# Attention with a Schraudolph-style exponent on VectorE: one of its four shifted lines made by DMA transfers inside SBUF

## The chip, the cores and the metric

The kernel runs on one core of a Trainium2 chip. The metric is the time of one execution on the device, in microseconds (us). Three executions of the kernel before took 676.72, 677.89 and 678.13 us, so the median is 677.89 us. A further execution was profiled: it took 677.84 us, and its span, from the first to the last instruction of the program, is 675.9 us.

Engine names are those of the profile: PE is TensorE (matrix multiply), ACT is ScalarE, DVE is VectorE, POOL is GpSimd and SP is SyncE, which here only issues DMA transfers. PEld is the weight load of PE.

## The reference

Attention without a mask over 32 heads, 2048 queries and keys, and 20 numbers per head. Queries and keys are normalised, a temperature per head scales the logits, and all is bf16:

```python
qn = q / (jnp.sqrt((q * q).sum(axis=-1, keepdims=True)) + eps)
kn = k / (jnp.sqrt((k * k).sum(axis=-1, keepdims=True)) + eps)
logits = jnp.einsum('bhqd,bhkd->bhqk', qn, kn) * t[None, :, None, None]
attn = _softmax(logits, axis=-1)
return jnp.einsum('bhqk,bhkd->bhqd', attn, v)
```

q, k and v are (1, 32, 2048, 20), t is (32). Since the logits are bounded by t, no maximum is subtracted: the kernel computes exp(logit) for each pair, multiplies it with v, and divides by the sum, which comes from a column of ones beside v.

## The kernel before, in words

**Tiles.** The work is cut into units: one head, 128 keys (on the partitions) and 512 queries (on the free axis). There are 32 heads x 16 key blocks x 4 query blocks = 2048 units. Four heads make a group (8 groups), a group and a query block make a superblock (32 superblocks of 64 units). PE makes the logits of a unit in a PSUM bank of 128 x 512, an engine takes the exponent and writes it to SBUF in 16 bits, and PE multiplies that tile with v into the accumulator `psO`.

**Two ways to an exponent.** A unit goes one of two ways.

- An *A unit* goes to ACT. PE puts two or three units ("a wave") into `psA`, and one ACTIVATE (line 867) writes exp of all of them into `pA`. A unit costs PE one multiplication with v.
- A *D unit* goes to DVE (and POOL). Line 313 (`P1`) multiplies and adds a constant and writes int16 to `dI`, so that the bits read as float16 are roughly an exponential. Three more lines of the same unit, `dS1`, `dS2` and `dS3`, are `dI` plus an integer constant each (`SHIFTS`; the constant of `dS3` is 565 - 123 = 442). The four readings, with `dI` counted once whole and once half through `vhalf`, are summed by PE in `psO`, and their errors cancel. A D unit costs PE five multiplications with v.

In the kernel before 1448 units are A units and 600 are D units. D units do not start before 12% of the work is issued (`D_FROM`).

**The shifts.** `shift_op` (line 318) makes a shifted line on DVE (line 328, up to four tiles of 512 in one instruction, `RUN_MAX`) or on POOL (line 326, 512 int16 as 256 int32, or two tiles at once). POOL is given only `dS1` (`POOL_S` = 1); DVE makes all of `dS2` and `dS3` and what POOL does not reach of `dS1`. `dI` and `dS1` to `dS3` are rings of 20 tiles (`RING`).

**The order of work.** A planner in the kernel (`make_plan`, line 423) plays the execution before it is built: it has a cost for each instruction, lets each engine take the ready piece of work of the best priority, and writes down the order of every engine. That order is fixed in the program; the engines meet only through semaphores. What is an A unit and what a D unit comes out of this play: `step_qkd` (line 916) starts a D unit when a bank of `psD` is free and no more than 24 shifts are waiting (`D_WAIT`). Two neighbouring `P1` are joined into one instruction if 12 or more shifts are waiting (`JOINB`, line 1035). If PE is used little, it gets filler multiplications (line 542) that add zeros.

The planner keeps POOL and DVE apart. Every DVE operation is marked `port` unless it is one of `P1`, `cp`, `drain`, `red`, `inv`, `rec` (line 207); `step_pool` (line 1052) starts a POOL instruction only while a DVE instruction without that mark runs, and only if it fits into it; a POOL instruction sets `lock`, until which DVE takes no marked one. An operation with `alone` set (line 1056) is exempt: it starts on POOL as soon as it is ready, and sets no lock.

SP issues its transfers in its order too: loads of q, k, v (80 KB to 320 KB), transposes of the padded q and k inside SBUF (`tr_op`, line 394: 128 rows of 4 KB, so 512 KB), and stores of the output.

Of the kernel before, what the change touches and what calls it, by code (L numbers as in the profile page):

```python
# [10 lines left out]
I16 = mybir.dt.int16  # L11
# [5 lines left out]
SHIFTS = (123, 382, 860, 565)  # L17
# [9 lines left out]
WAVES = (3, 2)  # L27
NPA = 14
RING = 20
RUN_MAX = 4  # L30
RUN_MIN = 4
D_FROM = .12
D_END = 14
D_LAST = 14
# [98 lines left out]
def bass_standalone__qk_norm__prompt_kernel(  # L133
# [12 lines left out]
    NSB = HG * QG  # L146
    QW = 512

    with ExitStack() as es:
        sbuf = lambda name, shape, dt: es.enter_context(nc.sbuf_tensor(name, shape, dt))  # L150
        sem = lambda name: es.enter_context(nc.semaphore(name))
# [10 lines left out]
        qpad = [sbuf(f"qpad{i}", [128, R, NH, 32], BF16) for i in range(2)]  # L162
# [6 lines left out]
        dI = sbuf("dI", [128, RING * QW], I16)  # L169
        dS = [dI] + [sbuf(f"dS{i}", [128, RING * QW], I16) for i in range(1, len(SHIFTS))]  # L170
        zt = sbuf("zt", [128, QW], BF16)
        shc = sbuf("shc", [128, len(SHIFTS)], I32)
        nrc = sbuf("nrc", [128, 4], F32)
        iot = sbuf("iot", [128, 128], F32)
        idn = sbuf("idn", [128, 128], BF16)
        nr0 = sbuf("nr0", [128, 2, NH, 4], F32)
# [17 lines left out]
            return dma_sems[nsem[0] - 1]  # L194

        n_sq = [0]

        def ap(tile, base, *dims):
            return bass.AP(tile, base.offset, [base.ap[0]] + [list(d) for d in dims])
# [118 lines left out]
        def shift_op(eng, i, j, n):  # L318
# [3 lines left out]
            if eng == "POOL":  # L322
# [4 lines left out]
            return dve(f"S{i}", n * QW, R4,  # L327
                       lambda e: e.tensor_single_scalar(o, x, float(SHIFTS[i] - SHIFTS[0]), ALU.add), rd, wr)  # L328

        def half_op(hg):  # L330
            b = hg % 2
            f = lambda tl: tl[b][:, :, :, :].rearrange("p h r d -> p (h r d)")
            return dve("vh", NH * R * 32, R4, lambda e: e.tensor_single_scalar(f(vhalf), f(vaug), 0.5, ALU.mult),  # L333
                       [("v", b, hh) for hh in range(NH)] + [("vz", b)], [("vh", b)])
# [88 lines left out]
        def make_plan(share):  # L423

            P = Plan()
            nsem[0] = n_sq[0] = 0
            SWITCH, PEL, SEML = 0.11, 0.18, 0.06
            units_of = lambda sb: {hh: [(sb, hh, r) for r in range(R)] for hh in range(NH)}
            pool = {sb: units_of(sb) for sb in range(NSB)}
            left = lambda sb: sum(len(x) for x in pool[sb].values())  # L430
# [18 lines left out]
            seq = [0]  # L449
            lock = [0.0]  # L450
            sp_todo = []
            pool_todo = []
            pending_pv = []
            shifts = []
            pe_mode, grp, pe_t = None, [0.0] * 4, 0.0

            def ready_at(op):
# [59 lines left out]
            o = P.link(load_qk(0, 0, 0)[0])  # L517
# [19 lines left out]
                    want_dve(o, 1.5)  # L537
            for o in zeros(1, [("qpad", 0, 0)]):
                want_dve(o, 5)

            def heat_mm(bank, n):
                return lambda e: e.matmul(bank, zt[:, 0:128], zt[:, 0:n], start=False, stop=False, skip_group_check=True)  # L542
# [38 lines left out]
            for r0, r1, a0, a1 in ((4, 16, 1, 2), (4, 16, 0, 1)):  # L581
# [28 lines left out]
            def progress():  # L610
                return (issued_a + issued_d) / float(R * NH * QG)
# [16 lines left out]
            def feed_prep():  # L628
                while next_prep:
                    pr, o = next_prep[0]  # L630
                    if pr is None:
                        for w_ in ("k", "q"):
                            x = tr_op(o, w_, 0, R)
                            x.reads.append((w_ + "z", o % 2))
                            want_sp(x)
                        next_prep.pop(0)
                        continue
                    if progress() < pr:
                        break
                    want_dve(o, PRIO)  # L640
                    next_prep.pop(0)
# [274 lines left out]
            def step_qkd(used, with_a):  # L916
                nonlocal a_sb, d_sb, issued_d, d_over
                if d_over or progress() < D_FROM:
                    return False
                d_sb = a_sb  # L920
                if a_sb == NSB or a_sb == NSB - 1 and left(a_sb) < D_END:
                    d_over = True
                    return False
                while d_sb < NSB - 1 and left(d_sb) < D_LAST:
                    d_sb += 1
                if d_sb == NSB - 1 and left(d_sb) < D_END or left(d_sb) < D_LAST:
                    return False
                if pe_mid:
                    return False
                def empty(i):  # L930
                    rds = P.readers.get(("psD", i), [])
                    return all(r.done is not None and r.done + SEML <= now for r in rds) and (rds or P.last_w.get(("psD", i)) is None)
                pb = issued_d % 2
                if not empty(pb):
                    return False
                n = 2 if not pb and left(d_sb) > 1 and empty(1) else 1
                if len(shifts) > D_WAIT:
                    return False
                j = issued_d % RING
                old = [(nm, j + t_) for t_ in range(n) for nm in ["dI"] + [f"dS{i}" for i in range(1, len(SHIFTS))]]  # L940
                if any(x[3] in old for x in pending_pv):
# [12 lines left out]
                pe_group("QKD", [qk_mm(u, psD[:, (pb + i) * QW:(pb + i + 1) * QW]) for i, u in enumerate(us)], "qk",  # L954
                         [kk for u in us for kk in qk_keys(u)], [("psD", pb + i) for i in range(n)], [u[1] for u in us])
                p1s = [p1_op(pb + t_, j + t_, 1) for t_ in range(n)]
                for t_, p1 in enumerate(p1s):
                    want_dve(p1, PRIO1)
                    for i in range(1, len(SHIFTS)):

                        shifts.append((issued_d - n + t_, i, j + t_, 1, p1))
                for t_, u in enumerate(us):
                    for i, cs in enumerate(COEF):
                        nm = f"dS{i}" if i else "dI"
                        x = dS[i][:, (j + t_) * QW:(j + t_ + 1) * QW].bitcast(F16)
                        for c in cs:
                            pending_pv.append((p1s[t_] if i == 0 else Later(nm, j + t_, issued_d), u, x, (nm, j + t_), c != 1))
                return True

            def step_act():  # L970
                nonlocal n_act
# [141 lines left out]
            while True:  # L1113
                moved = True
                while moved:
                    moved = False
                    feed_prep()
                    if loaded < HG and progress() > loaded - 1 + (0.02 if loaded > 1 else 0.2) and cur >= (loaded - 1) * QG:
# [172 lines left out]
```

## Time and profile before

| what | value |
|---|---|
| median of three executions | 677.89 us |
| profiled execution | 677.84 us |
| span of the profiled execution | 675.9 us |
| granted TensorE clock | 0.996 |
| ACT busy | 662.3 us (98%) |
| DVE busy | 657.4 us (97%) |
| PE busy | 653.6 us (97%) |
| POOL busy | 345.6 us (51%) |
| mean busy share of the DMA engines, queue q1 | 18.6% |

The busy time of an engine is the union of its instructions; a matmul's end is modelled, so PE's share is not a measure of its peak. A row of the groups gives the line of the code, the engine, the operation, what it writes and reads, shapes, the count, then the busy time in us and the mean duration in ns (durations of neighbours overlap a little, so busy divided by count is what one more costs), then the idle time in front of the group and what ended it. The page also follows the chain of work that ended last back from the end, and gives its shares by engine and line.

### The profile page before, as it was taken

To read this page: it belongs to the slowest core of one execution; us is meant where nothing else is said; L and a number is where in the kernel's file an instruction comes from. 1 tells how busy PE (TensorE), PEld (TensorE's weight loads), DVE (VectorE), ACT (ScalarE), POOL (GpSimd) and SP (SyncE) were. 2 spreads that over 40 slices of the span, in tenths; PEclk is the share of its full clock that TensorE was granted. 3 is DMA by queue.
4 is the path that set the end of the run, shared out by engine and by line. 5 is a ranking of instruction groups with operands and counts; after the bars stand their busy time and mean duration, and the time that the engine had idled before them with its cause. 6 is when DMAs were issued, how large, how long until landed. Compare 5 with 4: busy or idle time off the path is not lost.

```text
span 675.9 us, 17317 instructions
## 1 busy us (share of the span) xinstructions
PE 653.6 (97%) x7454; PEld 214.0 (32%) x7454; DVE 657.4 (97%) x1049; ACT 662.3 (98%) x587; POOL 345.6 (51%) x533
## 2 busy tenths in 40 slices
PE   8999999999999999999999999999999999999996
PEld 4433323323333222232323232323232323232232
DVE  7999999999999999999999999999999999999994
ACT  6999999999999999999999999999999999999996
POOL 3364455454654545545355545655456554546652
PEclk8999999999999999999999999999999999999999
DMA  6500133005130043000530014300133001100000
GB/s 68 86 7 1 33 73 39 1 2 102 9 33 1 13 92 20 21 2 10 94 21 21 1 33 72 21 21 2 32 57 35 22 1 36 30 7 16 2 11 15
DMA packets 113778, 19.66 MB, mean 29 GB/s; under 512 B 102944, under 2 KB 113696, under 8 KB 113696
## 3 DMA queue, kind: packets, MB, share of 16 engines
q1 hardware_dynamic: 112896, 18.37, 18.6%
q8 instruction: 60, 0.98, 0.6%
q10 hardware_dynamic: 800, 0.12, 0.1%
q14 instruction: 22, 0.18, 0.1%
HBM read 7.87 MB, written 2.62 MB: 16 GB/s over the span
## 4 chain that ended last, share of the span: by engine, by line
ACT 68%; PE 25%; DVE 6%; DMA 0%; issue 0%; POOL 0%; DVEq 0%
ACT pA L867 68%; PE psO L696 11%; PE psA L674 8%; PE psO L542 3%; PE psD L674 3%; DVE dI L313 3%; DVE dS L328 1%; DMA qk<-in_q_dram 0%; DVE ssum L247 0%; DVE accT L348 0%; DVE vhalf L333 0%; DVE sqs L244 0%; DVE qpad L292 0%; DVE rn L279 0%; POOL kpad L292 0%
## 5 line engine op out<-in xcount | busy, mean ns | idle before, releaser
L867 ACT ACTIVATE pA<-psA 128x1536 bf16<-128x1536 f32 x579 | 658.1, 1323 | 3.7 <-PE psA L674 3.1
L326 POOL TENSOR_TENSOR dS<-dI,shc 128x256 int32<-128x256 int32 (+1 forms) x369 | 265.5, 723 | 223.4 <-DVE dS L328 170.6
L313 DVE TENSOR_SCALAR dI<-psD 128x512 int16<-128x512 f32 (+1 forms) x414 | 370.8, 916 | 3.7 <-PE psD L674 1.3
L674 PE MATMUL psA<-qT,kT 32*128 32x512 bf16 x1724 | 250.1, 383 | 12.4 <-ACT pA L867 9.4
L696 PE MATMUL psO<-dS,vaug 128*32 128x512 f16 x1800 | 248.5, 383 | 0.0
L696 PE MATMUL psO<-pA,vaug 128*32 128x512 bf16 x1448 | 242.9, 384 | 0.0
L328 DVE TENSOR_SCALAR dS<-dI 128x2048 int16<-128x2048 int16 (+3 forms) x366 | 227.3, 644 | 0.0
L674 PE MATMUL psD<-qT,kT 32*128 32x512 bf16 x600 | 167.9, 381 | 2.0 <-DVE dI L313 1.1
L696 PE MATMUL psO<-dI,vaug 128*32 128x512 f16 x600 | 136.6, 385 | 0.5 <-DVE accT L348 0.5
L696 PE MATMUL psO<-dI,vhalf 128*32 128x512 f16 x600 | 134.9, 382 | 0.0
L674 PEld LDWEIGHTS psA<-qT,kT 32*128 32x128 bf16 x1724 | 62.0, 91 | 207.7 <-ACT pA L867 187.2
L696 PEld LDWEIGHTS psO<-dS,vaug 128*32 128x32 bf16 x1800 | 65.1, 95 | 91.6 <-issue 65.0
L696 PEld LDWEIGHTS psO<-pA,vaug 128*32 128x32 bf16 x1448 | 62.0, 94 | 44.4 <-issue 27.7
L542 PE MATMUL psO<-zt 128*128 128x128 bf16 x659 | 64.1, 225 | 0.0
L542 PEld LDWEIGHTS psO<-zt 128*128 128x128 bf16 x659 | 40.3, 99 | 40.4 <-issue 40.0
L674 PEld LDWEIGHTS psD<-qT,kT 32*128 32x128 bf16 x600 | 37.2, 91 | 28.6 <-DVE dI L313 18.5
L292 POOL TENSOR_TENSOR qpad<-qk,rn 128x160 bf16<-128x160 bf16 x56 | 24.8, 459 | 35.6 <-DVE dS L328 27.6
L292 POOL TENSOR_TENSOR kpad<-qk,rn 128x160 bf16<-128x160 bf16 (+1 forms) x57 | 25.6, 463 | 32.2 <-DVE dS L328 28.6
L696 PEld LDWEIGHTS psO<-dI,vaug 128*32 128x32 bf16 x600 | 34.2, 94 | 23.2 <-issue 11.6
L696 PEld LDWEIGHTS psO<-dI,vhalf 128*32 128x32 bf16 x600 | 34.8, 95 | 14.9 <-issue 10.8
L354 POOL TENSOR_TENSOR ost<-accT,rec 128x320 bf16<-128x320 f32 x31 | 23.7, 766 | 25.8 <-DVE dS L328 22.6
L348 DVE STREAM_TRANSPOSE accT<-psO 128x512 f32<-128x512 f32 x32 | 22.5, 702 | 5.4 <-PE psO L696 5.4
(54 smaller groups left out, 114.6 us busy)
## 6 DMA issues: line engine op xcount, KB each, us to landing
vaug<-in_v_dram SPq DMA_DIRECT2D x32, 80.0 KB, 4.1
qk<-in_k_dram SPq DMA_DIRECT2D x7, 320.0 KB, 4.4
out_dram<-ost SPq DMA_DIRECT2D x28, 80.0 KB, 1.9
qk<-in_q_dram SPq DMA_DIRECT2D x6, 320.0 KB, 4.3
qk<-in_q_dram SPq DMA_DIRECT2D x4, 80.0 KB, 3.2
out_dram<-ost SPq DMA_DIRECT2D x7, 40.0 KB, 2.0
qk<-in_k_dram SPq DMA_DIRECT2D x1, 240.0 KB, 3.7
qk<-in_q_dram SPq DMA_DIRECT2D x1, 240.0 KB, 4.3
```

What stands on the lines that cost most here:

```text
L292: emit = lambda e, o=dst, x=src, s=sc: e.tensor_tensor(o, x, s, ALU.mult)
L313: lambda e: e.tensor_scalar(dst, psD[:, pb * QW:(pb + n) * QW], 1024.0 * LOG2E, 15360.0 - 1024.0 * LOG2K + SHIFTS[0], ALU.mult, ALU.add),
L326: lambda e: e.tensor_tensor(o.bitcast(I32), x.bitcast(I32), c, ALU.add), rd + ["shc"], wr)
L328: lambda e: e.tensor_single_scalar(o, x, float(SHIFTS[i] - SHIFTS[0]), ALU.add), rd, wr)
L348: dve("drain", QW, R1, lambda e: e.transpose(aT[:, :, :].rearrange("p b d -> p (b d)"), psO[:, :]), ["psO"], [("accT", b)]),
L354: pool_op("omul", 320, True, lambda e: e.tensor_tensor(dst, num, rcb, ALU.mult), [("accT", b), ("rec", b)], [("ost", ob, qg)]) if pool else
L542: return lambda e: e.matmul(bank, zt[:, 0:128], zt[:, 0:n], start=False, stop=False, skip_group_check=True)
L674: return lambda e: e.matmul(dst, lhsT, rhs, tile_position=(32 * hh, 0))
L696: return lambda e: e.matmul(dst, lhsT, rhs, start=first, stop=last, skip_group_check=True, tile_position=(0, 32 * hh))
L867: a = Op("ACT", "exp", lambda e, s=src, d=dst: e.activation(d, s, ACT.Exp), [("psA", slot)], [("pA", pslot, i) for i in range(WAVES[slot]) ...
```

## The change

The line `dS3` of most D units is no longer made by DVE. For each batch of four neighbouring tiles of the ring (`DB` = 4):

1. `set`: SP issues a transfer SBUF to SBUF that copies `cadd`, a tile of 128 x 2048 int16 filled once with the constant 442, over the four tiles of `dS3`. It can run as soon as the old contents of the tiles have been read.
2. `far`: once the four tiles of `dI` are written and `set` has landed, POOL issues a transfer SBUF to SBUF that adds `dI` onto those four tiles (`accum_op=ALU.add`).

A batch is made so if at least 24 units are left in the superblock (`DMA_LEFT`) and it is not the last one; otherwise DVE makes `dS3` as before. `far` is `alone`: the planner lets POOL issue it whenever it is ready. The planner counts `DMA_POOL` for the issue and `DMA_LAT` until it lands, and 4.0 for `set` (figures written in the code, see the diff, not measurements). PE's multiplications with `dS3` of these tiles wait for the semaphore of `far`.

Since the planner plays the work with the new costs, the whole order comes out anew. By the instructions of the two programs (the branch that runs):

| instructions | before | after |
|---|---|---|
| A units / D units | 1448 / 600 | 1424 / 624 |
| ACTIVATE of 3 / 2 / 1 units | 290 / 289 / 0 | 285 / 284 / 1 |
| `P1` of one tile / of two | 228 / 186 | 510 / 57 |
| DVE shifts of 4 / 3 / 2 / 1 tiles | 291 / 31 / 33 / 11 | 169 / 46 / 72 / 51 |
| POOL shifts of one tile / of two | 272 / 97 | 307 / 26 |
| `set` on SP, `far` on POOL | 0 | 126 each, all of four tiles |
| PE multiplications with `dI`, `dS` and `pA` | 4448 | 4544 |
| PE filler multiplications (line 542 before) | 659 | 315 |

So 504 of the 624 tiles of `dS3` come from transfers.

```diff
+DB = 4
+DMA_POOL = 1.05
+DMA_LAT = 4.0
+DMA_LEFT = 24
+DMA_EVERY = 1
+DMA_ALONE = True
...
+        cadd = sbuf("cadd", [128, DB * QW], I16)
...
+        def shared(o, name, j):
+
+            k = (name, j // DB)
+            if k not in ring_sems:
+                ring_sems[k] = sem(f"s_{name}{j // DB}")
+            ring_val[k] = ring_val.get(k, 0) + 16
+            o.sem, o.val = ring_sems[k], ring_val[k]
+            return o
+
+        def far_op(j, n):
+            i = len(SHIFTS) - 1
+            sl = slice(j * QW, (j + n) * QW)
+            o = Op("POOL", "far", lambda e: e.dma_start(dS[i][:, sl], dI[:, sl], accum_op=ALU.add), [("dI", j + t_) for t_ in range(n)] + [("set", j)],
+                   [(f"dS{i}", j + t_) for t_ in range(n)], DMA_POOL, DMA_POOL + DMA_LAT)
+            o.alone = DMA_ALONE
+            return shared(o, "far", j)
+
+        def set_op(j, n):
+            i = len(SHIFTS) - 1
+            sl = slice(j * QW, (j + n) * QW)
+            return shared(Op("SP", "set", lambda e: e.dma_start(dS[i][:, sl], cadd[:, 0:n * QW]), ["cadd"],
+                             [("set", j)] + [(f"dS{i}", j + t_) for t_ in range(n)], 0.1, 4.0), "set", j)
...
+            if share:
+                want_dve(Op("POOL", "z", lambda e: e.memset(cadd[:, :], SHIFTS[-1] - SHIFTS[0]), [("qpad", 0, 0)], ["cadd"], 1.8, 1.9), 5)
...
                 for t_, p1 in enumerate(p1s):
                     want_dve(p1, PRIO1)
-                    for i in range(1, len(SHIFTS)):
+                    batch = (issued_d - n + t_) // DB
+                    if (j + t_) % DB == 0:
+                        far[0] = left(d_sb) >= DMA_LEFT and d_sb < NSB - 1 and batch % DMA_EVERY == 0 and RING % DB == 0
+                        if far[0]:
+                            want_sp(set_op(j + t_, DB))
+                    elif far[0] and lates and lates[0][1] != d_sb or d_sb == NSB - 1:
+                        far[0] = False
+                    if far[0]:
+                        lates.append((j + t_, d_sb))
+                    for i in range(1, len(SHIFTS) - far[0]):
...
+            def feed_far():
+                while lates and (len(lates) >= DB or not far[0] or left(lates[0][1]) < D_LAST):
...
+                    o = P.link(far_op(j, k))
...
+                    pool_todo.append([0, seq[0], o])
+                    del lates[:k]
```

More of the change, by code (lines that the diff above doesn't have):

```diff
@@ L196, in bass_standalone__qk_norm__prompt_kernel @@
         n_sq = [0]
+        ring_sems, ring_val = {}, {}
         def ap(tile, base, *dims):
@@ L426, in make_plan @@
             nsem[0] = n_sq[0] = 0
+            ring_val.clear()
             SWITCH, PEL, SEML = 0.11, 0.18, 0.06
@@ L454, in make_plan @@
             shifts = []
+            lates, far = [], [False]
             pe_mode, grp, pe_t = None, [0.0] * 4, 0.0
@@ L940, in step_qkd @@
                 old = [(nm, j + t_) for t_ in range(n) for nm in ["dI"] + [f"dS{i}" for i in range(1, len(SHIFTS))]]
+                old += [(f"dS{len(SHIFTS) - 1}", t_) for t_ in range((j + n - 1) // DB * DB, (j + n - 1) // DB * DB + DB) if t_ >= j]
                 if any(x[3] in old for x in pending_pv):
@@ L968, in step_qkd @@
                 return True
+            def feed_far():
+                while lates and (len(lates) >= DB or not far[0] or left(lates[0][1]) < D_LAST):
+                    j, sb_ = lates[0]
+                    k = 1
+                    while k < min(DB, len(lates)) and lates[k] == (j + k, sb_):
+                        k += 1
+                    o = P.link(far_op(j, k))
+                    for y in pending_pv:
+                        if y[3][0] == f"dS{len(SHIFTS) - 1}" and j <= y[3][1] < j + k:
+                            y[0].op = o
+                    seq[0] += 1
+                    pool_todo.append([0, seq[0], o])
+                    del lates[:k]
             def step_act():
@@ L1117, in make_plan @@
                     feed_prep()
+                    feed_far()
                     if loaded < HG and progress() > loaded - 1 + (0.02 if loaded > 1 else 0.2) and cur >= (loaded - 1) * QG:
```

## The prediction

> **What bounds the kernel now.** I read the page's busy times first, then the chain of work that ended last, then the groups with shapes apart, and last the stretches.
>
> ```profile
> PE 653.6 (97%) x7454; PEld 214.0 (32%) x7454; DVE 657.4 (97%) x1049; ACT 662.3 (98%) x587; POOL 345.6 (51%) x533
> ...
> ACT 68%; PE 25%; DVE 6%; DMA 0%; issue 0%; POOL 0%; DVEq 0%
> ...
> L867 ACT ACTIVATE pA<-psA 128x1536 bf16<-128x1536 f32 x579 | 658.1, 1323 | 3.7 <-PE psA L674 3.1
> ```
>
> ACT carries 68% of the chain and waits for PE only 3.7 us in front of its exponents. The stretches (columns: sum, then busy time and count of PE, PEld, DVE, ACT, POOL) show that DVE is as full:
>
> ```profile
> 200.00:300.00 100.00, 97.20 (x1137) 31.00 (x1135) 99.36 (x153) 99.83 (x89) 50.65 (x73) 1.00 0.15 25
> ```
>
> So the time is the work of exponents and shifts divided between ACT and DVE, both without a gap. It falls only if units move from ACT to DVE and DVE has room for them. The prices, by shape:
>
> ```profile
> L313 DVE TENSOR_SCALAR dI<-psD 128x1024 int16<-128x1024 f32 x186 | 225.5, 1212 | 3.1 <-PE psD L674 1.3
> L328 DVE TENSOR_SCALAR dS<-dI 128x2048 int16<-128x2048 int16 x291 | 195.8, 690 | 0.0
> L326 POOL TENSOR_TENSOR dS<-dI,shc 128x256 int32<-128x256 int32 x272 | 165.1, 611 | 130.3 <-DVE dS L328 96.2 <-DVE dI L313 19.6 <-DVE sqs L244 8.8
> L313 DVE TENSOR_SCALAR dI<-psD 128x512 int16<-128x512 f32 x228 | 145.3, 675 | 0.6 <-PE psA L674 0.4
> L326 POOL TENSOR_TENSOR dS<-dI,shc 128x512 int32<-128x512 int32 x97 | 100.5, 1037 | 93.1 <-DVE dS L328 74.3 <-DVE rsa L272 3.8 <-DVE sqs L244 3.3
> L542 PE MATMUL psO<-zt 128*128 128x128 bf16 x659 | 64.1, 225 | 0.0
> L328 DVE TENSOR_SCALAR dS<-dI 128x1536 int16<-128x1536 int16 x31 | 17.3, 559 | 0.0
> L328 DVE TENSOR_SCALAR dS<-dI 128x1024 int16<-128x1024 int16 x33 | 14.0, 433 | 0.0
> L328 DVE TENSOR_SCALAR dS<-dI 128x512 int16<-128x512 int16 x11 | 3.2, 288 | 0.0
> ```
>
> **The sum, part by part.** It is made against the profiled execution, 677.84 us (span 675.9, so 1.9 lie around it), 0.05 under the median of 677.89.
>
> *ACT.* 658.1 / 1448 units = 0.4545 us a unit; 24 units fewer are 10.9 us. ACT is the chain, so this counts in full: -10.9.
>
> *DVE.* One `P1` costs 145.3 / 228 = 0.637 us, a joined one 225.5 / 186 = 1.212. After: 510 x 0.637 + 57 x 1.212 = 394.1, against 370.8 now: +23.3. Shifts of 4, 3, 2, 1 tiles cost 0.673, 0.558, 0.424, 0.291 (busy by count); 169, 46, 72 and 51 of them are 184.7, against 230.3: -45.6. DVE's 657.4 becomes 635.1 in a span of about 665. Its idle time rises from 18.5 to 30, so in sum DVE does not bind. Half of what the transfers take from it is spent again, on `P1` that are no longer joined and on `dS1` tiles that leave POOL (466 tiles before, 359 after).
>
> *POOL.* Its shifts cost 307 x 0.607 + 26 x 1.036 = 213.3 against 265.6. The 126 `far` issues are not in this trace. SP's issues, the nearest rows, take 0.43 us (a load) to 2.05 us (a transpose), so 54 to 258 us in all; I take 1.05, the code's figure, inside these bounds: 132. The memset of `cadd` is about 2 us (the 128x768 memset takes 0.74). POOL comes to 345.6 - 52.3 + 132 + 2 = 427 us, 64%: room in sum. But POOL works in order, and the next `dS1` shifts and output scalings stand behind each `far`, which waits for `set` and four `P1`.
>
> *SP.* 126 `set` issues at about 0.5 us (its load issues) are 63 us, and SP is mostly idle. They are interleaved with transposes that wait there for POOL's `qpad` (233.1 us in all): a `set` behind one could be late. In the order only one to three per group stand close behind a transpose, so I charge nothing.
>
> *PE.* 24 more D units are 96 more multiplications; hidden by fillers, which fall from 659 (64.1 us) to 315 (about 31). With half the cushion, I let ACT wait for PE twice as long as now: +3.7 (bounds: nothing, and 7.4, as much again).
>
> *Landing.* Between the issue of a `far` and its first reader on PE the order puts 4 ACTIVATEs in 12 batches, 5 in 40, 6 in 21, 7 or more in 53. At 658.1 / 579 = 1.137 us each that is a budget of 4.5, 5.7, 6.8 and 8.0 us. What must fit, from rows:
>
> ```profile
> q1 hardware_dynamic: 112896, 18.37, 18.6%
> ...
> out_dram<-ost SPq DMA_DIRECT2D x28, 80.0 KB, 1.9
> ...
> kT<-kpad SPq DMA_TRANSPOSE x8, 4.4
> ```
>
> The transpose moves the same 512 KB inside SBUF in 4.4 us. In the trace's DMA records a packet of 160 bytes takes 14 ns and one of 640 bytes 32 ns, so 0.0375 ns a byte and some 162 ns for a row of 4 KB; each of 16 engines has 8 rows, 1.3 us. The 80 KB store spends 0.26 of its 1.9 us so, so about 1.6 is fixed. A copy then lands in 2.9 us. The add needs two tiles where a copy needs one, so it is between one copy (2.9) and twice the moving part (4.2); 4.4, the transpose, closes the bound. With the issue, 4.0 to 5.3 us, middle 4.65: over the budget only in the 12 tightest batches, 12 x 0.15 = +1.8 (bounds 0 and 12 x 0.8 = 9.6).
>
> The Trainium skill, page "Collectives: The Full Stack", section "The bandwidth ceiling: the fold count and why AG ≠ RS ≠ AR", says that a reducing transfer goes at half a copy's rate because it has two sources to read. By that rule the landing is the upper 5.3 us and the sum 7.8 us longer; no run shown has an adding transfer.
>
> *Sum of the likeliest case:* 677.84 - 10.9 + 3.7 + 1.8 = 672.4 us; by its bounds 666.9 to 677.8 less the unlikely meeting of all upper ends, say 667 to 676.
>
> **Rival 1: the issue of a `far` holds up DVE (slower).** DVE's int16 shifts and POOL's work exclude each other in this trace, and the planner's `alone` lets `far` start without regard to it. At 662.67 us of the span the output scaling on POOL began inside a DVE shift, and the next shift came while it ran:
>
> ```profile
> 662.54 1.88 DVE L328 TENSOR_SCALAR dS<-dI 128x2048 int16<-128x2048 int16 x2
> 662.67 1.20 POOL L354 TENSOR_TENSOR ost<-accT,rec 128x320 bf16<-128x320 f32 x1
> ```
>
> ```profile
> L328 DVE TENSOR_SCALAR dS<-dI x366: 276/682/1235, 25.6 to 664.7; 128x2048 int16<-128x2048 int16 x145, 128x1024 int16<-128x1024 int16 x20, 128x1536 int16<-128x1536 int16 x15, 128x512 int16<-128x512 int16 x3
> ```
>
> ```profile
> L354 POOL TENSOR_TENSOR ost<-accT,rec x31: 747/751/1200, 41.7 to 662.7; 128x320 bf16<-128x320 f32 x31
> ```
>
> The two longest of their kind (min/median/max in ns) are these two: the scaling took 1200 ns instead of 751, the shift behind it 1235 instead of 682, ending 0.55 us after POOL did. Everywhere else the order keeps them apart. If issuing a transfer holds the same resource, then with 338 shifts in 665 us (0.51 a us) an issue of 1.05 us meets 0.53 shifts, each held for half the issue to all of it: 126 x 0.53 x (0.53 to 1.05) = 35 to 70 us of DVE. Of this DVE's extra room takes 11.5, and the rest reaches ACT, as both are full: 672.4 + 23.5 to 58.5 = 696 to 731. It decides from 17 us of delay on, 0.13 us an issue: the 11.5 us of room and the 5.4 gained. For it speaks that window; against it, that it shows arithmetic on POOL with tensors read and written, not an issue.
>
> The Trainium skill, page "SBUF — State Buffer", section "Who interferes with whom", makes this a rule: VectorE's two-port modes and GpSimd share one port pair as an exclusive lock, and a transfer issued from GpSimd has its descriptors written through it. The window agrees with the lock; for the issue no run shown has a case.
>
> **Rival 2: transfers land late (slower).** `set` and `far` come about every 5 us (126 between the first `P1`, at 24 us of the trace, and the last superblock, which begins near 31/32 of the span, 655 us). They keep the DMA engines busy for 126 x (2.6 to 3.9) = 328 to 491 us, beside 126 us (18.6%) of other queues: 68 to 93% of 667. If a `set` and the `far` in flight share the engines, each lands up to 1.3 us later, at up to 6.6 us: 12 x 2.1 + 40 x 0.9 = 61 us of waits on PE, 30 us at 6.0. That gives 700 to 732. For it: the loads of a group already fill half of some slices of the page. Against it: the mean is under full load, and a late `set` finds some slack on POOL.
>
> **Rival 3: a wash.** Waits of 4 to 7 us more than in the sum, by either way, leave 676.5 to 679.2: the same.
>
> **How the numbers follow.** The sum as planned, 42%: 672.4, its own range 667 to 676. Rival 1, 27%. Rival 2, 22%. A wash, 5%. Milder forms of rivals 1 and 2, 679 to 695, 4%. No change can be told within 0.2%, 676.5 to 679.2. So faster 0.42, same 0.05, slower 0.53: the single likeliest case is faster, but more often than not one of the two mechanisms spoils it. The range leaves out the upper parts of both rivals: 666 to 718.
>
> **What would show it.** If right: L867 falls to about 647 us, its idle time stays under 8, DVE's shifts keep a median near 0.68 us and few of them exceed 0.8, and PE's waits for `far` are under 10 us. Rival 1 shows as DVE shifts of 1 us and more beside each issue; rival 2 as PE (or POOL, for `set`) waiting tens of us for DMA, and a landing of 6 us and more. The forecast is also wrong if an issue on POOL takes much more than 1.05 us: at 2 us, POOL's `dS1` shifts behind it would leave their places beside `P1` and meet DVE's.

## The result, and the profile after

The changed kernel takes 802.97 us (median of four executions, 801.51 to 806.92) against 677.88 for the kernel before on the same chip: a ratio of 1.186, 95% interval 1.181 to 1.191. The forecast of 672.4 us and its range of 666 to 718 both miss. The profiled execution took 806.92 us, with a span of 805.1. Of the times below, those of `quiet0`, `ahead1` and `load_only` leave out one slower execution each, over 1.5% above the fastest of its kernel.

The first parts of the page of the kernel after (busy time and instructions of each engine; the granted clock and the DMA engines in 40 slices; queues; chain by engine, then by line; groups):

```profile
PE 720.6 (90%) x7248; PEld 209.6 (26%) x7248; DVE 659.6 (82%) x1174; ACT 664.5 (83%) x578; POOL 413.4 (51%) x624
...
PEclk9879996897888698989959999889989679778999
DMA  5786899769798688968969889988997979957820
...
q0 software_dynamic: 18144, 66.07, 43.5%
q1 hardware_dynamic: 131040, 84.44, 37.1%
...
PE 36%; DVE 30%; DMA 19%; SPq 6%; ACT 4%; issue 3%; POOL 1%; DVEq 0%; POOLq 0%
PE psO L731 18%; DVE dI L321 18%; DMA dS<-dI 15%; PE psA L709 11%; DVE dS L336 9%; SPq L422 5%; PE psD L709 5%; ACT pA L902 4%; DMA dS<-cadd 4%; PE psO L577 3%; DVE accT L379 1%; DVE vhalf L364 1%; SPq L358 0%; DVE ssum L255 0%; DMA qk<-in_q_dram 0%
...
L902 ACT ACTIVATE pA<-psA 128x1536 bf16<-128x1536 f32 (+1 forms) x570 | 660.2, 1267 | 128.7 <-PE psA L709 67.8
L321 DVE TENSOR_SCALAR dI<-psD 128x512 int16<-128x512 f32 (+1 forms) x567 | 396.9, 731 | 125.3 <-PE psD L709 119.5
```

ACT and DVE have about the busy time that they had before (664.5 and 659.6 us), but 128.7 us of idle time now stand in front of the exponents, where 3.7 stood. ACT has left the chain (4% instead of 68%). PE, DVE and transfers carry it. The queues q0 and q1 used 18.6% of the DMA engines before; now they use 81%, and the clock row stands at 5 to 8 tenths in half of its slices. The two rows of the page of the kernel before, for comparison:

```profile
PEclk8999999999999999999999999999999999999999
DMA  6500133005130043000530014300133001100000
```

Who waited for whom in the kernel after (columns: us in total, times, longest us):

```profile
DVE dI L321 <- PE psD L709: 119.5, 80, 7.8
ACT pA L902 <- PE psA L709: 67.8, 59, 6.4
ACT pA L902 <- PE psD L709: 58.8, 43, 8.3
PEld psO L731 <- DMA dS<-dI: 54.2, 34, 6.6
PE psO L731 <- DMA dS<-dI: 43.7, 22, 6.3
POOL dS L350 <- DMA dS<-cadd: 42.1, 19, 5.1
...
PE psD L709 <- issue: 18.9, 4, 7.7
```

ACT and DVE wait for PE. PE itself waits 43.7 us for adds that have not landed, and 18.9 us in four waits that the view puts down to "issue", each of which ended 0.09 us after a transpose of q had landed. POOL waits 42.1 us for copies, with its `dS1` shifts queued behind. The transfers of the kernel after (median us from issue to landing):

```profile
dS<-cadd SPq DMA_DIRECT2D x126, 512.0 KB, 4.9
dS<-dI POOLq DMA_DIRECT2D x126, 512.0 KB, 6.1
...
kT<-kpad SPq DMA_TRANSPOSE x8, 6.3
qT<-qpad SPq DMA_TRANSPOSE x8, 9.4
```

The transposes landed in 4.4 us before. In the trace's DMA records a 4 KB packet takes 161 ns in a copy and 336 ns in an add (medians). The adds fill each of the 16 engines for 347 us, the copies for 170, everything else on q1 for 129: 646 us of work for a kernel that was to last some 667.

These waits explain about half of the loss. PE stands idle for 84.5 us (805.1 - 720.6), 62 more than before (675.9 - 653.6 = 22.3), but the span is 129 us longer. The rest is the clock. The stretches of the kernel after around one wait (columns as in the stretches of before: sum, busy time and count of PE, PEld, DVE, ACT, POOL, clock, DMA share, GB/s; the share counts a packet whole where it starts, so it can pass 1):

```profile
380.00:390.00 10.00, 9.94 (x108) 3.05 (x106) 10.00 (x18) 10.00 (x9) 6.79 (x13) 1.00 1.03 165
390.00:400.00 10.00, 7.78 (x93) 2.12 (x87) 9.66 (x17) 9.47 (x9) 4.74 (x8) 1.00 0.95 259
400.00:410.00 10.00, 3.77 (x25) 0.66 (x25) 2.62 (x5) 1.10 (x2) 1.58 (x3) 0.57 0.90 195
410.00:420.00 10.00, 10.00 (x70) 1.88 (x70) 7.63 (x14) 6.62 (x6) 4.03 (x6) 0.50 0.45 121
420.00:430.00 10.00, 10.00 (x109) 2.88 (x101) 8.20 (x18) 8.51 (x8) 3.25 (x5) 0.91 0.97 197
430.00:440.00 10.00, 9.81 (x122) 3.02 (x119) 10.00 (x16) 10.00 (x10) 5.71 (x9) 1.00 0.93 184
```

The timeline of the same place (start, us, engine, line, operation, tiles, count, and in brackets the idle time before it):

```profile
396.16 0.39 PE L709 MATMUL psA<-qT,kT 32*128 32x512 bf16 x2
396.21 4.40 SPq L431 DMA_TRANSPOSE qT<-qpad  x1
...
406.23 0.58 PE L709 MATMUL psD<-qT,kT 32*128 32x512 bf16 x1 [7.65 <-issue]
406.74 0.61 PE L731 MATMUL psO<-dS,vaug 128*32 128x512 f16 x2
```

Here the transpose of the next group's q, issued at 396.2 us beside transfers, lands 9.9 us later. PE stands still for 7.65 us, and when it goes on, a multiplication takes 0.58 to 0.61 us instead of 0.38 (rows of several span overlapping ones): the clock is granted at half. For the next ten us PE shows busy all the time and gets 70 multiplications done instead of 110, so ACT runs 6.62 us of 10 although PE no longer waits. I cut the trace into stretches of 5 us. In the kernel before no stretch has a clock under 0.75. In the kernel after 38 of 161 have (the trace's clock records grant half for 198 us in all, against 7 before), and in them ACT stands idle for 82.7 us, out of 140.6 (805.1 - 664.5) over the whole span. The Trainium skill, "TensorE: Matmul & The Clock Gate", section "HAM oscillation — how this bites in real kernels", describes this: waits for DMA that are longer than a window of about 3.4 us put the array back to half clock each time. This trace agrees in the main (0.38 us before the wait, 0.61 after it), but half the clock was also granted at 445.8 us, 1.2 us after a wait of only 2.0 us, and here the clock records show half the clock from 401.4 to 421.9 us, so for 15.6 us after PE went on; why it lasted so long is open. The transfers themselves don't lower the clock: it is 1.00 at a DMA share of 1.03, from 380 to 390 us.

### The profile page after: what moved, and what is told of

It reads as the page before. It is cut to its first block, busy times and chain, and to the rows that moved or that the text cites. A ratio compares the mean times of both kernels' runs of the same rounds, so it can differ in the third digit from the quotient of the medians.

```text
span 805.1 us, 17326 instructions
## 1 busy us (share of the span) xinstructions
PE 720.6 (90%) x7248; PEld 209.6 (26%) x7248; DVE 659.6 (82%) x1174; ACT 664.5 (83%) x578; POOL 413.4 (51%) x624
## 4 chain that ended last, share of the span: by engine, by line
PE 36%; DVE 30%; DMA 19%; SPq 6%; ACT 4%; issue 3%; POOL 1%; DVEq 0%; POOLq 0%
PE psO L731 18%; DVE dI L321 18%; DMA dS<-dI 15%; PE psA L709 11%; DVE dS L336 9%; SPq L422 5%; PE psD L709 5%; ACT pA L902 4%; DMA dS<-cadd 4%; PE psO L577 3%; DVE accT L379 1%; DVE vhalf L364 1%; SPq L358 0%; DVE ssum L255 0%; DMA qk<-in_q_dram 0%
## 5 line engine op out<-in xcount | busy, mean ns | idle before, releaser
L902 ACT ACTIVATE pA<-psA 128x1536 bf16<-128x1536 f32 (+1 forms) x570 | 660.2, 1267 | 128.7 <-PE psA L709 67.8
L321 DVE TENSOR_SCALAR dI<-psD 128x512 int16<-128x512 f32 (+1 forms) x567 | 396.9, 731 | 125.3 <-PE psD L709 119.5
L334 POOL TENSOR_TENSOR dS<-dI,shc 128x256 int32<-128x256 int32 (+1 forms) x333 | 218.6, 678 | 230.2 <-DVE dI L321 107.0
L731 PE MATMUL psO<-dS,vaug 128*32 128x512 f16 x1872 | 284.4, 416 | 43.7 <-DMA dS<-dI 42.0
L709 PE MATMUL psA<-qT,kT 32*128 32x512 bf16 x1742 | 271.8, 418 | 5.3 <-ACT pA L902 3.0
L731 PE MATMUL psO<-pA,vaug 128*32 128x512 bf16 x1424 | 268.1, 420 | 2.0 <-DMA dS<-dI 1.7
L709 PE MATMUL psD<-qT,kT 32*128 32x512 bf16 x624 | 221.8, 420 | 25.4 <-issue 18.9
L336 DVE TENSOR_SCALAR dS<-dI 128x2048 int16<-128x2048 int16 (+3 forms) x338 | 194.8, 600 | 0.0
L350 POOL DMA_DIRECT2D dS<-dI x126 | 119.0, 947 | 92.3 <-DMA dS<-cadd 42.1
L577 PE MATMUL psO<-zt 128*128 128x128 bf16 x315 | 42.9, 258 | 0.0
L300 POOL TENSOR_TENSOR kpad<-qk,rn 128x160 bf16<-128x160 bf16 (+1 forms) x57 | 26.8, 473 | 26.7 <-DVE dS L336 18.6
```

The costliest lines, as they stand in the source:

```text
L300: emit = lambda e, o=dst, x=src, s=sc: e.tensor_tensor(o, x, s, ALU.mult)
L321: lambda e: e.tensor_scalar(dst, psD[:, pb * QW:(pb + n) * QW], 1024.0 * LOG2E, 15360.0 - 1024.0 * LOG2K + SHIFTS[0], ALU.mult, ALU.add),
L334: lambda e: e.tensor_tensor(o.bitcast(I32), x.bitcast(I32), c, ALU.add), rd + ["shc"], wr)
L350: o = Op("POOL", "far", lambda e: e.dma_start(dS[i][:, sl], dI[:, sl], accum_op=ALU.add), [("dI", j + t_) for t_ in range(n)] + [("set", j ...
L709: return lambda e: e.matmul(dst, lhsT, rhs, tile_position=(32 * hh, 0))
L731: return lambda e: e.matmul(dst, lhsT, rhs, start=first, stop=last, skip_group_check=True, tile_position=(0, 32 * hh))
```

## The experiments

Theories when they began: the bytes of the transfers fill the DMA engines, so that everything on them is late (rival 2, larger than priced); the issue of a `far` holds up DVE (rival 1); the new order itself is worse.

The second was settled without a run. In the kernel after, DVE shifts of four tiles that overlap only a `far` issue on POOL take 687 ns on average (58 cases, longest 812); with nothing on POOL 680 ns (77 cases); beside a POOL tensor operation alone 811 ns (23 cases); 11 more met both, 1113 ns. So an issue does not hold DVE here; arithmetic on POOL does.

**Fewer bytes, same order.** The transfers keep their number, place and waits, but move 256 of 2048 columns of a batch, so most of `dS3` isn't made. `thin_both` thins copy and add from the sixth batch on, `thin_add` only the add, `thin_set` only the copy (its adds read zeros), and `thin_early` thins every add, copies from the sixth on.

```diff
-            sl = slice(j * QW, (j + n) * QW)
+            n_far[0] += 1
+            sl = slice(j * QW, j * QW + (n * QW if n_far[0] <= WHOLE else min(n * QW, FAR_W)))
```

> Leaves out: from the sixth batch on, both transfers move only the first 256 of their 2048 columns, so dS3 is stale or wrong there. Every instruction, its place and its waits are as in the changed kernel. Theory L (load: the bytes of the transfers fill the DMA engines, 81% busy over 805 us, so transfers land late): the adding transfer lands in about 3 us, the DMA engines fall under 30%, no wait of PE for it over 5 us in all, and the time is what the order allows without them, 668 to 678 us. Theory O (order: the new order, the issues on POOL and the waits cost by themselves, whatever the bytes): 780 to 805 us, as the changed kernel. Theory C (the lower granted clock, 0.88, comes first and makes PE late): the clock stays under 0.92 and the time over 740 us.

> Leaves out: from the sixth batch on the adding transfer moves 256 of 2048 columns, the copy all. Theory L: the adding transfer has 347 of the 646 us that the 16 engines spend on packets, on average, and 304 of them go; the engines fall to about 50% and the time to 670 to 690 us. If the copies (and SP, which issues them in order behind transposes) are what is late, POOL still waits for them some 40 us in all and the time stays over 720 us.

> Leaves out: from the sixth batch on the copy moves 256 of 2048 columns, and the adding transfer adds a tile of zeros of the same size, so dS3 is wrong. The adding transfer moves all its bytes. Theory L: of 646 us of packets 149 go, which leaves 497, some 70 to 75% of the engines; adds land in about 5 us instead of 6.1, and the time is between, 690 to 750 us. If the copies are what is late: under 690 us.

> As the run with both transfers thin, but the adds are thin from the first batch on; only the first five copies are whole. Leaves out most of dS3 in the same way. If the 9 us by which that run missed 672.4 come from the five whole adds at the start, among the first loads (they landed in 7.4 us; ACT was 3.7 us less busy in the first 50 us than before the change): 676 to 679 us. If they come from the order itself: 680 to 683 us as there.

| kernel | time, us | ratio to before (95%) | clock | lands, add / copy |
|---|---|---|---|---|
| thin_both | 681.56 | 1.0067 (1.0047 to 1.0087) | 0.987 | 2.5 / 1.9 |
| thin_add | 686.42 | 1.0132 (1.0112 to 1.0153) | 0.981 | 2.9 / 3.8 |
| thin_set | 751.71 | 1.1096 (1.1062 to 1.113) | 0.921 | 5.1 / 3.4 |
| thin_early | 676.66 | 0.9994 (0.9983 to 1.0004) | 0.993 | 2.5 / 1.9 |

With the same instructions in the same order, 121 us of the loss go when the bytes go, though `thin_both` (668 to 678 expected) and `thin_set` (690 to 750) came out above their ranges. The first line of the page of `thin_both`:

```profile
PE 656.2 (97%) x7248; PEld 202.6 (30%) x7248; DVE 644.1 (95%) x1174; ACT 653.8 (96%) x578; POOL 413.4 (61%) x624
```

The adds alone make most of it: taking their bytes away saves 117 us, taking the copies' away 51. The two together are more than the whole; that one late transfer makes others late would explain it, but was not measured apart. The change also halved PE's fillers (659 to 315), but that is not what lowers the clock: `thin_both` has the same 315 and a clock of 0.987. The five whole adds at its start are all that sets `thin_both` apart from `thin_early`, which took 4.9 us less.

The page of `thin_early` also shows that the gain isn't there even with transfers that cost nearly nothing:

```profile
PE 652.2 (97%) x7248; PEld 201.9 (30%) x7248; DVE 643.3 (95%) x1174; ACT 653.1 (97%) x578; POOL 412.2 (61%) x624
...
DVE 40%; ACT 33%; PE 24%; issue 1%; DMA 0%; POOL 0%; DVEq 0%
```

ACT's busy time falls by 9.2 us (662.3 to 653.1) as promised, but its idle time rises from 13.6 to 21.0, so the span falls by 1.8. DVE and PE now take turns with ACT in the chain. Of the 7.4 us, 2.5 stand at 550 to 600 us, where the clock is 0.93, 2.2 at 250 to 350, and 3.4 from 600 us on; the rest cancels. What in the order costs these us was not tried.

**Fewer batches, or longer due times.** `every2` gives only every second batch to transfers. `budget1` keeps all, but the planner counts 7 us for the add and 6 for the copy.

```diff
-DMA_EVERY = 1
+DMA_EVERY = 2
```

```diff
-DMA_LAT = 4.0
+DMA_LAT = 7.0
...
-                             [("set", j)] + [(f"dS{i}", j + t_) for t_ in range(n)], 0.1, 4.0), "set", j)
+                             [("set", j)] + [(f"dS{i}", j + t_) for t_ in range(n)], 0.1, 6.0), "set", j)
```

> DMA_EVERY = 2, the full result: every second batch is made by transfers (58 instead of 126), with a new order, 608 D units. Theory L: packets take 129 + 58/126 x 517 = 367 us of the engines, 54%; landing near its minimum, adds in about 5 us; the time 670 to 700 us, and whether it beats 677.9 depends on the few batches that fall together with the loads of a group. Theory O: half of the loss remains, 735 to 745 us.

> DMA_LAT = 7.0 instead of 4.0 and 6.0 instead of 4.0 for the copy: the planner counts on the landings that the changed kernel's trace shows (6.1 and 4.9 us in the median), so PE, POOL and the units are ordered around them. Still every batch (121 transfers of each kind), 617 D units. Theory L1 (the engines are full): the bytes do not change, packets alone take 129 + 121/126 x 517 = 625 us of a span of about 675, so landings go on growing and the time stays over 730 us. Theory L2 (only the order's budget was too small): 672 to 690 us.

`every2` took 700.86 us (1.0355, 1.0332 to 1.0379), `budget1` 740.65 (1.0925, 1.0834 to 1.1017). The one leaves 24 us of the loss, the other 63, and neither cures it. In `budget1` PE's waits for adds fell to 19.9 us, but the add now lands in 6.7 us, the copy in 5.6, and POOL still waits 42.8 us for copies: full engines take part of what the plan allows more.

**Both, and the copies asked earlier.** `budget2` has every second batch from the tenth on, with the longer due times (57 batches; the planner also counts 0.5 us instead of 0.1 for issuing a copy, there and in the runs derived from it). `ahead2` is the same with the copy asked one batch earlier, `ahead1` that with every batch.

```diff
+            def feed_set():
+                b = next_set[0]
+                if b is None or b in early or d_over or b * DB - issued_d > DB or a_sb >= NSB - 1:
+                    return
...
+                want_sp(set_op(s0, DB))
```

> Every second batch, the first ten batches left to DVE (so that no transfer meets the first loads), and the longer budget of 7.0 and 6.0 us: 57 transfers of each kind, 610 D units. Theory L (the loss is transfers that land after their budget): the adds land in about 5 us, well inside, PE waits for them under 3 us in all, and 18 units fewer on ACT than with no change beyond 600 D units, 10 x 0.4545 = 4.5 us, bring 671 to 676 us. Theory O (the issues on POOL and the waits cost by themselves): 685 us and more.

> As the run with every second batch and the longer budget, but the copy of a batch is asked for one batch earlier (as soon as the old tiles have been read), so that it may be late by 3.5 us in the median before POOL waits; some copies (15 of 71) turn out not to be needed. 56 adds, 608 D units. Theory H (what that run lost is copies that stand on SP behind a transpose: at 89.3 us of its span the issue of one took 9.0 us, POOL waited 9.6 us for the copy behind it, and ACT stood for some 8 us): 676 to 681 us, POOL's waits for copies under 2 us in all. If the engines' load as such costs: 685 us and more, as there.

> The same for every batch, the first ten left to DVE (118 adds, 142 copies, 619 D units; budget 7.0 and 6.0 us); to be held against the run with every batch and that budget, 740.7 us. Theory H: POOL's wait for copies (42.8 us there) falls under 10 us and the time under 715 us. Theory L (full engines): packets take 129 + 118 x 2.75 + 142 x 1.37 = 648 us of the engines, so whatever is asked for earlier the transfers go on queuing, and the time stays at 725 to 760 us.

`budget2` took 687.19 us (1.014, 1.0123 to 1.0157) where 671 to 676 were expected (for 10 units fewer on ACT; the "18" there is a slip), `ahead2` 687.72 (1.0162, 1.0144 to 1.0181). In `ahead2` POOL no longer waits for copies, and the time is the same: the wait of `far` for `set` was not the loss. `ahead1` took 798.60 us (a second execution, the profiled one, 811.71) where 725 to 760 were expected: no better than the change, and 58 us over `budget1`. Its profile shows POOL's waits for copies down to 17.9 us, but the transposes of q landed in 12.7 us (median) instead of 7.0, and PE's waits that ended with one rose from 17.7 to 39.8 us. With the engines full, the earlier copies (142 for 118 adds) moved the lateness to other transfers.

**Load without a reader.** In `load_only` DVE and POOL make all lines, and the transfers fill a scratch that nobody reads.

```diff
-            o = Op("POOL", "far", lambda e: e.dma_start(dS[i][:, sl], dI[:, sl], accum_op=ALU.add), [("dI", j + t_) for t_ in range(n)] + [("set", j)],
-                   [(f"dS{i}", j + t_) for t_ in range(n)], DMA_POOL, DMA_POOL + DMA_LAT)
+            o = Op("POOL", "far", lambda e: e.dma_start(scr[:, sc], dI[:, sl], accum_op=ALU.add), [("dI", j + t_) for t_ in range(n)] + [("set", j)],
+                   [("scr", j // DB % 2)], DMA_POOL, DMA_POOL + DMA_LAT)
```

> DVE and POOL make all shifted lines as before the change; the transfers (107 of four tiles and 4 of two, of each kind) go to a scratch tile that nobody reads, with the same issues on POOL and SP. The planner makes 552 D units with POOL busier, so ACT has 1496 units, 48 more than before the change, 48 x 0.4545 = 21.8 us. Theory R (only readers that wait for late transfers lose): 677.9 + 21.8 = 700, within 694 to 706 us, at a DMA share of about 80%. Theory X (the load itself also hurts, through transposes and loads that land late, or the clock): 715 us and more.

It took 782.27 us (a second execution, the profiled one, 803.31). This does not separate what it was made for: the scratch has two slots, and so brought waits of its own (POOL 96.7 us for copies, SP 462.7 us for adds, DVE's `P1` 52.2 us for adds that still read `dI`). It shows only that no multiplication has to read a transferred line for the time to rise some 80 us above the 700 that its units cost.

**Are the transposes the sore spot?** In `budget2` one stretch stood out: a transpose of k issued at 80.4 us took 17.0 us to land. So `quiet` is `budget2` without the batches begun between 0.56 and 0.97 of a group's work, so that hardly a transfer meets a transpose; `clash` leaves out as many elsewhere. `mid2` keeps the transposes of the middle groups under transfers and leaves out the beginning and the end. `quiet0` and `quiet1` put `quiet`'s rule on the changed kernel and on `budget1`.

```diff
-                        far[0] = left(d_sb) >= DMA_LEFT and d_sb < NSB - 1 and batch % DMA_EVERY == 0 and batch >= 10 and RING % DB == 0
+                        far[0] = left(d_sb) >= DMA_LEFT and d_sb < NSB - 1 and batch % DMA_EVERY == 0 and batch >= 10 and not .56 < progress() % 1 < .97 and RING % DB == 0
```

In `clash` the added condition is `not .06 < progress() % 1 < .47`; in `mid2` `batch >= 10` becomes `1.0 < progress() < 7.2`.

> As budget2 (every second batch of four tiles from the tenth on, longer due times in the plan), but no batch is given to transfers that is begun between 0.56 and 0.97 of a group's work, so that no copy or add is in flight while the next group's kT and qT are transposed. 35 batches, 608 units on VectorE. The longest losses of budget2 stood where transposes were issued beside transfers: a kT transpose took 17.0 us from issue to landing, and the exponents ran 2.29 us of the following 10. Theory Q (the transposes are what the transfers hurt at half load): the kT and qT of every group land within 5 us, no stretch of 50 us between 100 and 600 loses over 1 us of exponents, and the time is 674 to 679, as 8 units fewer on ScalarE are 3.6 us. Theory E (it is the order with joined tiles broken up, or the transfers wherever they stand): 681 to 686.

> The counterpart of quiet: the same rule, but the batches begun between 0.06 and 0.47 of a group's work are left out, so that nearly as many transfers (36 batches, 603 units on VectorE) stand around the transposes and the group change. Five units more on ScalarE than quiet are 2.3 us. Theory Q: transposes land 6 us and more after their issue in some groups, the exponents lose tens of us there, and the time is 684 to 692, at least 6 us over quiet. Theory E: within 4 us of quiet.

> As budget2, but transfers only from the first group change on and up to 7.2 groups of 8 (49 batches, 609 units on VectorE), so beside the transposes of six groups, and not in the stretch of 80 to 100 us and near the end, where budget2 and clash lost their time. Theory Q (transfers beside any transpose cost time): 683 or more, as in budget2 with 57 batches. Theory S (two single stretches lose it, the transposes of the middle groups stand it): 672 to 677, ScalarE at 49.5 us or more of exponents in every 50 us from 100 to 600.

> The changed kernel with its own due times, but without the batches begun between 0.56 and 0.97 of a group's work: 81 batches left of 126, at the full rate in the rest of each group, 616 units on VectorE. Theory L (at the full rate the engines are full wherever it stands): the loss goes by the batches, (802.97 - 677.88 + 10.9) / 126 = 1.08 us each, so 81 x 1.08 - 7.3 (16 units) = 80 over before, about 758, with the granted clock near 0.92 in the stretches with transfers and 1.0 in the others. Theory Q (most of the loss stands at the group changes): under 700.

> As quiet0 with the longer due times of budget1 (add 7 us, copy 6 us in the plan): 77 batches, 616 units. budget1 lost 740.7 - 677.9 + 10 = 73 us with 121 batches, 0.6 us each. Theory L: 77 x 0.6 - 7.3 = 39 over before, about 717. Theory Q: 671 to 682, near quiet.

Loss per batch is (time - before + 0.4545 x D units gained) / batches, before being that of the same runs; ACT idle is span less busy time; low stretches are those of 5 us with a clock under 0.75.

| kernel | batches | D units gained | time, us | ratio (95%) | loss per batch, us | ACT idle, us | low stretches |
|---|---|---|---|---|---|---|---|
| before | 0 | 0 | 677.88 | | | 13.6 | 0 of 135 |
| after | 126 | 24 | 802.97 | 1.186 (1.181 to 1.191) | 1.08 | 140.6 | 38 of 161 |
| quiet0 | 81 | 16 | 750.28 | 1.110 (1.104 to 1.116) | 1.00 | 86.5 | 20 of 149 |
| budget1 | 121 | 17 | 740.65 | 1.093 (1.083 to 1.102) | 0.58 | 82.8 | 15 of 148 |
| quiet1 | 77 | 16 | 712.99 | 1.055 (1.052 to 1.058) | 0.57 | 49.8 | 10 of 141 |
| every2 | 58 | 8 | 700.86 | 1.036 (1.033 to 1.038) | 0.48 | 33.5 | 6 of 139 |
| clash | 36 | 3 | 690.84 | 1.018 (1.017 to 1.020) | 0.40 | 28.0 | 4 of 137 |
| budget2 | 57 | 10 | 687.19 | 1.014 (1.012 to 1.016) | 0.24 | 25.7 | 4 of 136 |
| mid2 | 49 | 9 | 680.59 | 1.007 (1.004 to 1.010) | 0.16 | 19.1 | 1 of 135 |
| quiet | 35 | 8 | 674.45 | 0.9955 (0.994 to 0.997) | 0.01 | 14.2 | 0 of 134 |

Three things follow.

At the full rate it is mostly not the transposes. In `quiet0` they land in 4.3 us as before the change, and a batch still costs 1.00 us. The times forecast from the loss per batch (758 and 717) came within 8 us. The longer due times halve that loss, the half rate does too, and both together bring it to about a quarter (`budget2`, which also spares the first ten batches).

At the half rate the transposes are not the sore spot either, or only once. `clash` lost its time in two places, and at the other group changes, with transfers beside the transposes, ACT ran 49.4 to 50 us of every 50. So the expectations for `clash` and `quiet` came in by their numbers and not by their reason, the transposes. The first place, stretches of `clash` from 80 us on:

```profile
80.00:85.00 5.00, 5.00 (x57) 1.57 (x56) 5.00 (x9) 4.89 (x6) 2.37 (x6) 1.00 1.18 80
85.00:90.00 5.00, 2.71 (x33) 0.81 (x29) 4.57 (x6) 4.50 (x4) 2.04 (x4) 0.92 1.04 78
90.00:95.00 5.00, 0.83 (x10) 0.37 (x14) 0.00 (x0) 0.00 (x0) 0.00 (x0) 0.50 1.29 71
95.00:100.00 5.00, 5.00 (x46) 1.05 (x38) 2.94 (x3) 2.47 (x2) 1.94 (x2) 0.55 1.03 295
```

An add issued 0.1 us before a transpose landed in 14.8 us, the transpose in 17.0, on engines that were busy all the time and moved only 71 to 80 GB/s. The add's 4 KB packets took 830 ns on average there instead of 345, the transpose's 256-byte packets 70 instead of 21. The same pair stood as close at 404 and 488 us, and landed in 6.2 to 8.1 us. What is special at 80 us was not found.

The second place has hardly a transfer in it. Stretches of `mid2`, which has the same near the end:

```profile
630.00:635.00 5.00, 4.01 (x40) 1.26 (x36) 5.00 (x10) 4.98 (x5) 3.87 (x7) 1.00 0.02 3
635.00:640.00 5.00, 3.67 (x32) 0.82 (x28) 3.58 (x6) 4.34 (x5) 1.97 (x3) 0.75 0.37 82
640.00:645.00 5.00, 5.00 (x50) 1.60 (x47) 0.00 (x0) 2.21 (x2) 0.00 (x0) 0.57 0.10 20
```

PE has 32 to 40 multiplications where some 55 are usual, the clock falls, and ACT and DVE run dry, at a DMA share of 0.02 to 0.37. So it is more likely the order. The timeline of `mid2` shows the end of a superblock there:

```profile
634.14 3.57 DVE L336 TENSOR_SCALAR dS<-dI 128x512 int16<-128x512 int16 x5
637.63 0.70 DVE L379 STREAM_TRANSPOSE accT<-psO 128x512 f32<-128x512 f32 x1
```

DVE makes five shifts in a row (3.57 us from 634.14 us on) before it reads `psO` out (`accT`), and until then PE can't begin the next sums and has only ACT's next units to multiply. The same five shifts stand in front of the same `accT` in `clash`. These few us are why `mid2` missed its range of 672 to 677. That was read, not tried with another order.

`quiet` beats both kernels. It is 3.4 us faster than before for 8 units, 0.42 us each, close to the 0.4545 of the forecast. Its stretches (DVE and ACT are the third and fourth pair) are as full as those of before, with a DMA share under a half:

```profile
200.00:300.00 100.00, 96.63 (x1109) 30.51 (x1101) 99.46 (x164) 99.92 (x89) 57.66 (x82) 1.00 0.46 103
300.00:400.00 100.00, 98.36 (x1139) 29.81 (x1137) 99.43 (x165) 99.79 (x89) 59.60 (x96) 1.00 0.45 93
```

## Why the prediction was wrong

**Landing, the step that failed.** It charged 1.8 us (at most 9.6), from 2.9 us for a copy and 4.0 to 5.3 with the issue for an add. As times on free engines these were right: the fastest copy landed in 2.9 us, the fastest add in 4.5. A 4 KB copy packet was put at 162 ns and took 161. But the step let every transfer meet free engines, while the medians were 4.9 and 6.1 us and the longest 10.2 and 10.9. In place of its 1.8 us PE waited 43.7 us for adds, and 18.9 us more for transposes of q, on which the step had nothing. The upper bound of the sum was also added up wrong: its own upper ends give 666.9 + 7.4 + 9.6 = 683.9 us, not 677.8.

**Rival 2 was the right mechanism at a wrong price.** It had 22% and at most 61 us of waits. Three things were missing. First, the load: it was put at 68 to 93% of 667 us, and the trace gives 646 us, 97%. The add is to blame: its packet takes 336 ns, 2.1 times a copy's, so a `far` fills the engines for 2.75 us and a `set` for 1.35, together above the upper end of 3.9. The Trainium skill, "Collectives: The Full Stack", section "The bandwidth ceiling: the fold count and why AG ≠ RS ≠ AR", which gives a reducing transfer half a copy's rate, agrees with the 2.1. Second, it charged only batches over their budget by a fixed lateness, where copies, adds and the group's transposes all landed late. Third, it let a wait cost its own length. Here a wait of a few us on PE also halves the clock for the stretch after it: `thin_both` has the same instructions and a span that is 126 us shorter (678.8); of these, PE's waiting explains 62 (84.5 less 22.6) and PE's slower running 64 (720.6 us busy against 656.2).

**SP, costed at nothing, was not nothing.** Its own issues took longer under load: 93.2 us for the `set` instead of 63, and 5.0 us (median) for a transpose of q instead of 1.8. Rows of before could not show that.

**DVE "does not bind".** The prices held: `P1` 396.9 us against 394.1, shifts 194.8 against 184.7. But `thin_early`, with almost free transfers, gains 1.8 us of span and not 5.4 of time. The sum of ACT was right in busy time (-9.2 against -10.9); ACT's idle time, which the forecast let rise by 3.7 us, rose by 7.4. A sum of busy times did not show where in the order the room lies.

**Right:** POOL's 427 us (413.4), with a `far` issue of 0.87 us (median) instead of 1.05; and rival 1's "against", that the window shows arithmetic and not an issue. Rival 1 itself, with 27%, fell, and with it the reading that an issue takes the same lock as arithmetic on POOL: 687 against 680 ns.

## What to carry to other kernels

Before work is moved from an engine to transfers, add up the packet times on the DMA engines over the stretch in which they fall, and compare that with the stretch itself: near full, as here with 97% of the planned time, a transfer's landing time on free engines says little, and the small transfers that the kernel already had come late as well. A stall of PE is to be priced with the half clock behind it, about twice its length here. A little of such a change may pay where all of it does not: 35 batches gained 0.45%, 126 cost 18.6%.

## What the runs showed of the hardware that I had not expected

- An adding transfer inside SBUF takes 336 ns for a 4 KB packet, a copying one 161, and these medians stay the same from 35 batches (336 and 160) to 126. What grows with the load is the time from issue to landing: 3.4 and 5.2 us in `quiet`, 4.9 and 6.1 in the kernel after (copy and add, medians).
- After a PE wait of 7.65 us the granted clock was 0.57 and 0.50 in the two stretches of 10 us that followed, and 0.91 in the third. In `mid2` thin work on PE (32 to 40 multiplications in 5 us) was followed by the same fall with hardly a transfer running.
- An SP instruction that issues a transfer takes longer when the engines are full: up to 2.65 us for a copy that takes 0.47 (median), and 9.0 us for the transpose of q behind the slow one in `clash`.
